# Attention and gated long convolution on one core: DMA transposes for the outputs of the later pairs, one cast for q and k, separate weight tiles for local pairs, and another order of the work

## Chip, core and metric

The kernel runs on one core of one Trainium2 chip. The metric is device time in microseconds; the kernel before takes 206.59 us (median of 3 runs, 206.18 to 206.97). Times of single operations below come from one profiled execution of it, whose span is 205.4 us. The engines are called PE (matmul; PEld is its weight loading), DVE (vector), ACT (scalar, with activation tables), POOL (GpSimd) and SP (the queue that issues most DMAs).

## What is computed

Batch 4, 8 heads, 768 positions, head width 64. Heads 0, 2 and 6 see all earlier positions ("full"); the others see the first 4 positions and a window of 64 ("local"). The attention output, heads side by side (768 x 512 for each batch), goes through a projection to three parts; the middle one is convolved circularly along the sequence with a filter, all three are multiplied, and the product is projected again.

```python
scores = scale * q @ k.T                  # masked: causal; local heads: sink or window
a = exp(scores - max); a = a / (sum(a) + 1e-9)
attn = a @ v                              # (B, H, S, D)
x = attn.transpose(0, 2, 1, 3).reshape(B, S, H * D)
x1, x2, x3 = split(x @ w_proj, 3)
x2_conv = irfft(rfft(x2, axis=1) * rfft(filter, axis=0), n=S, axis=1)
out = (x1 * x2_conv * x3) @ w_out
```

## The kernel before

**Units of work.** Two heads, h and h + 4, form a pair; the 16 pairs are numbered n = 0 to 15, four for each batch, in the order full-full, local-local, full-local, local-local (`PAIRS`, `KINDS`). Every step of a pair or a batch is a small named operation (`ops`), and the string `FAST` lists the names in the order in which they are issued. Each engine takes its own instructions in that order, and so does SP with its DMAs; there is no scheduler behind it. A suffix `/v`, `/s`, `/p` names the engine of a copy or an elementwise operation (DVE, ACT, POOL), and `@0` to `@3` names one of four PSUM slots of two banks. An operation waits, through semaphores, for what it reads and for the last users of the buffer that it writes.

**A pair.** `lq`, `lk`, `lv` load q, k and v from SP. `cq`, `ck`, `cv` cast to bf16 (`ev`, L963 to L971, makes all such copies). For n < 8 (`TURNED`) `T` transposes q and k on PE (L1340) and `E` copies them out of PSUM; from pair 8 on `T` is one DMA transpose from SP (L1350). `kx`, `ks`, `vx`, `vs` build the short key and value tiles of local heads. `sc` computes a chunk of scores (L1385; chunks n.0 to n.5 for full pairs, n.0 to n.2 for local, n.0 to n.4 for mixed ones); for the first four pairs `sb` adds the mask on PE (L1398), later `mk` and `mr` multiply it in on DVE. `ex` takes the exponential of a chunk on ACT into the weight tile `pT` (L1404). `at` is the weighted sum for one of the two heads (L1449), `rec` and `nm` divide by the row sum (L1455, L1463, L1466). `tn` transposes the pair's output, six 128 x 128 blocks, on PE (L1522), and `te` copies the blocks from PSUM to `xT`. `fd`, `fe` and, from pair 8, `fA`, `fS`, `fb`, `fr` fold the output for the transform; `W` transforms it (L1502 to L1510) and `We` copies it to `xh`.

**A batch.** `X` multiplies the transformed output with the middle part of the projection (L1553, six halves of four 128 x 512 matmuls), `Xe` copies that out, `pa`, `pb`, `pc` and the swap `sw` (a DMA from SP) multiply by the filter's spectrum. `x1` and `x3` are the two outer parts (L1588, half tiles of four 128 x 384 matmuls), `xs` and `g` take them up. `c` transforms back (L1618, halves of three 128 x 384 matmuls), `ce`, `cv` and `y` finish the convolution and the product. `o` is the output projection (L1645), `oe` its eviction, `st` the store. All four pairs of a batch must be in `xT` before its first `x1` or `x3` matmul.

**Setup.** `sin`, `cos`, `turns`, `angle`, `wrap` compute the transform tables; `lfilt`, `fold`, `F`, `H` the filter's spectrum; `lw0.*`, `lw1.*`, `lw2.*` load the three parts of the projection weights and `lwo` the output weights, all as casting DMAs from POOL. `blank` issues matmuls on zeros at the start. ACT loads an activation table where its function set changes.

**Buffers.** q and k tiles, key tiles and value tiles rotate over three, `pT` over two (even pairs one, odd pairs, which are the local ones, the other).

Of the kernel before, what the change touches and what calls it, by code (L numbers as in the profile page):

```python
# [10 lines left out]
BF16 = mybir.dt.bfloat16  # L11
# [16 lines left out]
W = 512  # L28
# [86 lines left out]
TURNED_BACK = (0, 1, 2, 3, 4, 5, 6, 7, 8, 9, 10, 11, 12, 13, 14, 15)  # L115
# [793 lines left out]
def patterned(  # L909
# [55 lines left out]
    def ev(out, in_):  # L965
        if now["engine"] == "v":
            nc.vector.tensor_copy(out=out, in_=in_)  # L967
        elif now["engine"] == "p":
            nc.gpsimd.tensor_copy(out=out, in_=in_)  # L969
        else:  # L970
            nc.scalar.copy(out=out, in_=in_)  # L971
# [795 lines left out]
```

## Time and profile before

| | |
|---|---|
| median of 3 runs | 206.59 us |
| profiled execution, span | 205.4 us |
| busy: PE, DVE, ACT, POOL | 183.4, 161.0, 143.8, 81.5 us |
| share of 16 DMA engines, hardware queue | 57.6% |
| score exponentials on ACT (68) | 59.8 us |
| x1 and x3 matmuls on PE (256) | 48.3 us |
| transposes of attention outputs on PE (96) | 7.8 us |

A stretch of the profile gives the time for which each engine was busy in it; matmuls are pipelined and overlap, so a busy PE is not PE at its peak. The chain of waits goes back from the last instruction, at each step to what released it. An idle engine costs nothing unless that chain passes through its wait.

### The profile page before, as it was taken

The page shows a single profiled execution, that of the slowest core. Times are in us where ns is not written, and L with a number is a line of the kernel's source. Part 1 is how long each engine was busy: PE and PEld are TensorE (multiplying, and loading weights), DVE is VectorE, ACT ScalarE, POOL GpSimd, SP SyncE. Part 2 cuts the span into 40 slices and gives each one's busy share as a digit, 9 for nine tenths or more (in the row PEclk, how much of TensorE's full clock was granted, in tenths as well). Part 3 has the DMA queues.
Part 4 walks back from the last instruction along what each step waited for, and adds up shares of the span by engine and source line. Part 5 has one row for each costly group of instructions (what it writes and reads, how often), then busy time and mean ns, then how long its engine had stood idle before and what let it go on. Part 6 is the DMA issues. An engine that isn't in the chain of part 4 may idle for free.

```text
span 205.4 us, 4423 instructions
## 1 busy us (share of the span) xinstructions
PE 183.4 (89%) x1718; PEld 107.1 (52%) x1718; DVE 161.0 (78%) x296; ACT 143.8 (70%) x199; POOL 81.5 (40%) x106
## 2 busy tenths in 40 slices
PE   0993999979699779989999999999999999999990
PEld 0443576545346355535655666555655866545540
DVE  4384563967678799988989998899999988689850
ACT  3959779959788958699939889666897623424521
POOL 3739716564050420192174326203354595040600
PEclk9997579999999999999999999999999999999997
DMA  5999999999923979901999998152013200022174
GB/s 160 305 303 341 198 265 226 257 238 261 238 59 79 229 150 217 223 3 49 277 221 233 231 269 161 37 118 49 5 66 142 105 0 2 3 51 102 73 292 162
DMA packets 74159, 32.87 MB, mean 160 GB/s; under 512 B 63507, under 2 KB 70419, under 8 KB 74131
## 3 DMA queue, kind: packets, MB, share of 16 engines
q1 hardware_dynamic: 71186, 29.63, 57.6%
q0 software_dynamic: 2944, 2.88, 8.3%
q8 instruction: 15, 0.25, 0.5%
q14 instruction: 14, 0.11, 0.2%
HBM read 24.64 MB, written 6.29 MB: 151 GB/s over the span
## 4 chain that ended last, share of the span: by engine, by line
PE 63%; ACT 16%; DVE 15%; issue 2%; DMA 1%; ACTq 0%; DVEq 0%
PE f_x_ps L1588 15%; PE f_X_ps L1553 10%; PE f_out_ps L1645 9%; PE f_c_ps L1618 7%; PE f_sc L1385 6%; ACT f_pT L1404 5%; PE f_att L1449 4%; PE f_blank_ps L1010 3%; DVE f_attn L1466 3%; PE f_qkT_ps L1340 2%; ACT f_qkT L971 2%; DVE f_fo L974 2%; ACT f_HAB L1205 2%; PE f_xt_ps L1522 2%; PE f_W_ps L1510 2%
## 5 line engine op out<-in xcount | busy, mean ns | idle before, releaser
L1404 ACT ACTIVATE f_pT<-f_sc 128x1024 bf16<-128x1024 f32 (+3 forms) x68 | 59.8, 921 | 7.2 <-PE f_sc L1385 5.1
L1588 PE MATMUL f_x_ps<-f_xT,f_wproj 128*128 128x384 bf16 x256 | 48.3, 327 | 1.0 <-ACT f_pT L1404 0.5
L1588 PEld LDWEIGHTS <-f_wproj 128*128 128x128 bf16 x256 | 23.1, 98 | 17.7 <-issue 2.6
L1385 PE MATMUL f_sc<-f_qkT 64*128 64x128 bf16 (+3 forms) x248 | 23.1, 258 | 1.9 <-DVE f_attn L1466 0.9
L974 POOL TENSOR_TENSOR f_fo<-f_attn 128x384 bf16<-128x384 bf16 x15 | 15.7, 1062 | 19.0 <-DVE f_attn L1466 12.7
L1645 PE MATMUL f_out_ps<-f_wout,f_gy 128*128 128x512 bf16 x96 | 22.9, 380 | 0.0
L1553 PE MATMUL f_X_ps<-f_wproj,f_xh 128*128 128x512 bf16 x96 | 22.7, 380 | 0.0
L974 POOL TENSOR_TENSOR f_gy<-f_conv,f_gy 128x768 bf16<-128x768 bf16 x7 | 11.5, 1668 | 22.9 <-issue 13.2
L1629 DVE TENSOR_TENSOR f_conv<-f_evs,f_c_ps 128x384 bf16<-128x384 f32 x32 | 16.4, 548 | 3.2 <-ACT f_evs L971 2.0
L1449 PEld LDWEIGHTS <-f_pT 128*128 128x128 bf16 x472 | 17.5, 101 | 2.5 <-DVE f_attn L1466 0.6
L1385 PEld LDWEIGHTS <-f_qkT 64*128 64x128 bf16 x248 | 10.4, 95 | 15.8 <-issue 12.3
L1618 PE MATMUL f_c_ps<-f_Gi,f_P 128*128 128x384 bf16 x96 | 18.2, 325 | 0.4 <-ACT f_evs L971 0.2
L1449 PE MATMUL f_att<-f_v_aug,f_pT 128*128 128x65 bf16 x392 | 18.2, 199 | 0.2 <-DVE f_attn L1466 0.2
L971 ACT CAST f_x1s<-f_x_ps 128x768 bf16<-128x768 f32 x14 | 11.3, 810 | 8.2 <-PE f_x_ps L1588 6.5
L969 POOL COPY f_v_x<-f_v_aug 64x520 bf16<-64x520 bf16 (+1 forms) x15 | 9.7, 648 | 18.5 <-ACT f_v_aug L971 11.0
L1340 PE MATMUL f_qkT_ps<-f_identity,f_qk_bf 128*128 128x128 bf16 x96 | 9.0, 242 | 8.6 <-ACT f_qk_bf L971 5.6
L967 DVE COPY f_qkT<-f_qkT_ps 128x768 bf16<-128x768 bf16 x7 | 6.7, 957 | 12.6 <-ACT f_qkT L971 6.3
L971 ACT COPY f_evs<-f_c_ps 128x384 f32<-128x384 f32 x16 | 7.7, 480 | 11.7 <-PE f_c_ps L1618 10.8
L1466 DVE TENSOR_TENSOR f_attn<-f_att,f_rec 128x768 bf16<-128x768 f32 x15 | 14.3, 956 | 1.1 <-DVE f_rec L1455 0.5
L1645 PEld LDWEIGHTS <-f_gy 128*128 128x128 bf16 x96 | 8.9, 98 | 10.2 <-issue 0.3
L971 ACT COPY f_o<-f_out_ps 128x1024 f32<-128x1024 f32 (+1 forms) x11 | 9.7, 907 | 6.2 <-PE f_out_ps L1645 6.2
L1553 PEld LDWEIGHTS <-f_xh 128*128 128x128 bf16 x96 | 8.9, 98 | 9.9 <-issue 0.4
(128 smaller groups left out, 354.9 us busy)
## 6 DMA issues: line engine op xcount, KB each, us to landing
f_v_f<-in_v_dram SPq DMA_DIRECT2D x32, 192.0 KB, 4.7
out_dram<-f_o SPq DMA_DIRECT2D x9, 512.0 KB, 3.1
f_qk_f<-in_k_dram SPq DMA_DIRECT2D x5, 384.0 KB, 5.5
f_qk_f<-in_q_dram SPq DMA_DIRECT2D x5, 384.0 KB, 4.8
f_qk_f<-in_q_dram SPq DMA_DIRECT2D x10, 192.0 KB, 4.2
f_qk_f<-in_k_dram SPq DMA_DIRECT2D x10, 192.0 KB, 4.0
f_wproj<-in_moe_w_proj_dram POOLq DMA_DIRECT2D x6, 256.0 KB, 12.0
out_dram<-f_o SPq DMA_DIRECT2D x6, 256.0 KB, 3.6
```

What stands on the lines that cost most here:

```text
L971: nc.scalar.copy(out=out, in_=in_)
L974: (nc.gpsimd if now["engine"] == "p" else nc.vector).tensor_tensor(out, a, b, op)
L1340: nc.tensor.transpose(ps[:, a, t * 128:(t + 1) * 128], qk_bf(n)[:, a, t].rearrange("p hh d -> p (hh d)"), identity())
L1385: nc.tensor.matmul(sc[:, bank, col:col + 128 * cnt], lhsT=keys, rhs=qkT(n)[rows, 0, 128 * i:128 * (i + cnt)], start=(col == 0 or not biase ...
L1404: nc.scalar.activation(out=pT(n)[:, c, :, 0:w], in_=held[f"sc.{n}.{c}"][:, :, 0:w], func=AF.Exp, scale=SCALE)
L1449: nc.tensor.matmul(att[:, hh, 65 * i:65 * i + 65], lhsT=pT(n)[:, c, bank, col:col + 128], rhs=values, start=(z == 0), stop=(z == len(here) ...
L1466: nc.vector.tensor_mul(attn(n).rearrange("p i hh d -> p hh i d"), rows[:, :, :, 0:64], held[f"rec.{n}"][:, :, :, None].to_broadcast([128, ...
L1553: nc.tensor.matmul(ps[:, u, :], lhsT=xh(b)[:, cc, chain, 128 * part:128 * part + 128], rhs=wproj()[:, cc, DM:2 * DM], start=(cc == 0), sto ...
L1588: nc.tensor.matmul(ps[:, s, 0:HS], lhsT=wproj()[:, cc, part * DM + cb * 128:part * DM + (cb + 1) * 128], rhs=xT(b)[:, cc, s * HS:s * HS + HS],
L1618: nc.tensor.matmul(ps[:, r, 0:HS], lhsT=P(b)[:, t, u, ch], rhs=Gi()[:, tile_no], start=(m == 0), stop=(m == 2))
L1629: fn(conv[:, half * HS:half * HS + HS], held[f"evs.{b}.{cb}"], held[f"c_ps.{b}.{cb}"][:, 1, 0:HS])
L1645: nc.tensor.matmul(ps[:, i % 2, :], lhsT=gy(b)[:, cb, i * 128:(i + 1) * 128], rhs=wout()[:, cb, :], start=(cb == 0), stop=(cb == NC - 1))
```

## The change

- `TURNED_BACK` loses pairs 8 to 14. For these seven `tn` is one DMA transpose from SP, from the attention output straight to `xT`, and `te` is gone; pairs 0 to 7 and 15 keep PE.
- For pairs 8 to 15 the loads of q and k write a layout with the two heads beside each other, and one `cqk` casts both in one flat copy of 128 x 1536, in place of `cq` and `ck` of 128 x 768 each with a rearranged source.
- `pT` of local pairs is a tile of half the size, and two of them alternate; full and mixed pairs share the other.
- `ev` has a letter `d`, a plain DMA from SP; the new list uses it for `vs2`, `ks15`, `vx13` and `vx15`. An operation `exp0` takes the exponential of one column. `APART` is empty and has no effect.
- `FAST` is another list throughout, with other engines for many copies and other places for the loads.

```diff
-TURNED_BACK = (0, 1, 2, 3, 4, 5, 6, 7, 8, 9, 10, 11, 12, 13, 14, 15)
+TURNED_BACK = (0, 1, 2, 3, 4, 5, 6, 7, 15)
...
+        elif now["engine"] == "d":
+            nc.sync.dma_start(out=out, in_=in_)
...
+    @op("exp0")
+    def _():
+        nc.scalar.activation(out=table(), in_=table(), func=AF.Exp)
...
     def pT(n):
-        return buf(f"pT.{n}", [128, 6, 2, W], BF16, f"pT{n % 2}")
+        if KINDS[PAIRS[n % HP]] == "LL":
+            return buf(f"pT.{n}", [128, 3, 2, W], BF16, f"pTl{n // 2 % 2}")
+        return buf(f"pT.{n}", [128, 6, 2, W], BF16, "pT0")
...
-                            nc.sync.dma_start(out=qk[:, a, hh],
+                            nc.sync.dma_start(out=qk.rearrange("p a h t d -> p (a h t d)").rearrange(
+                                                  "p (a t h d) -> p a t h d", a=2, t=NT, d=D)[:, a, :, hh],
...
+        if n >= TURNED:
+            @op(f"cqk{n}")
+            def _(n=n):
+                ev(qk_bf(n).rearrange("p a t h d -> p (a t h d)"),
+                   held[f"qk_f32.{n}"].rearrange("p a h t d -> p (a h t d)"))
```

The branch that `tn` of pairs 8 to 14 now takes was in the code before:

```python
nc.sync.dma_start_transpose(out=xT(b)[:, hp, :].rearrange("p (t s) -> p t s", t=NT),
                            in_=attn(n).rearrange("p t hh d -> p (t hh d)"))
```

Of the new list, the start, the stretch with the weights' loads, and the stretch around the outputs of pairs 8 to 11:

```diff
+mblank blank0@0 fcol1 par mtab0 lk1 table sin0 tcol tfrac ck0/s lq2 fcol0 turns2 angle0 ident ones1 T0.1@1 quarter
+mtab2 blank1@2 angle2 angle1 turns1 wrap1 turns0 lq1 wrap2 cq0/s E0.1/s T0.0 lk2 cq1/p wrap0 lk3 sin1 size kz0
+cq2/v E0.0/v T2.0@3 T1.0@0 sc0.3@2 sin2 E1.0/v cos1 mtab1 mtab3 btab blank2@1 E2.0/s ck1/v cos2 sb0.3 ex0.3 ck2/p
...
+cv3/v cv2/p vs2/d exp0 lk4 vx2/v ex2.2 ex2.0 at1.0@1 at1.1 rec1 nm1/v tn0@2 te0/v W0.1@3 Gh0 W0.0 sc2.1@0 sb2.1
...
+vs5/p lv4 lw0.1 X0.1.1@2 sc4.2@1 sc4.3@3 ex4.3 lw0.0 X0.1.0 pa0.0/v mk4.2 ex4.2 mk4.1 lw2.1 lw2.0 T6.0@0 E6.0/s
...
+cv0.1.1 We4/s cv0.1.0 c0.0.0 ce0.0/v cqk10/s cv0.0.0 at6.0@0 cv0.0.1 T10 T9 vx6/p vs6/p at6.1 rec6 sc8.3@3 ex8.3
+c0.3.1@1 nm6/v c0.3.0 lwo ce0.3/s y0.1/p sc8.2@2 ex8.2 y0.0/p cv0.3.0 cv0.3.1 y0.3/p c0.2.0@3 c0.2.1 fd6/p sc8.4@0
+ce0.2/s sc8.0@2 vs7/v ex8.0 x30.3.1@1 x30.3.0 cv0.2.0 lk12 cv0.2.1 y0.2/v tn6@2 ex8.4 te6/s at7.0@3 lq12 g0.3 at7.1
+lk11 o0.1.0@0 sc8.5@2 ex8.5 rec7 kx9/v sc8.1@1 fe6/v nm7/v mk8.2 fd7/v ex8.1 mk8.0 o0.0.0 mk8.1 o0.1.1 o0.0.1
...
+mk11.2 mk11.1 x31.0.1 T12 We8/s sc12.0@0 sc12.5@3 rec10 nm10/v fe10/p fd10/v ex12.0 tn9 x11.2.0@2 x11.2.1 g1.0
+xs1.2/s lk13 at11.1@0 fr9 ex12.5 at11.0 rec11 x31.1.0@1 tn10 sc12.4@2 sc12.1@3 nm11/v x31.1.1 W9.0@0 lk15 pc1.2/v
+ex12.4 g1.1 tn11 W9.1 x31.2.1@2 ex12.1 We9/s mk12.2 sc12.2@1 fA10/v sc12.3@3 lq14 fS10/v fe11/p fr10 fd11/v ex12.2
+x31.2.0 g1.2 fA11/p c1.1.0@0 fb10/v fS11/v ex12.3 x12.0.0@1 pb1.0/v pc1.0/v x12.0.1 xs2.0/s x32.0.1@2 x32.0.0
+fb11/v fr11 W10.0@3 W10.1 ce1.1/s c1.1.1 g2.0 cv1.1.0 We10/s lq13 cqk13/p lv12 lk14 cv1.1.1 c1.0.0@1 c1.0.1 ce1.0/v
+cv1.0.1 cv1.0.0 W11.1@2 cv13/s W11.0 We11/s cv12/s cqk14/s T13 cqk15/p y1.1/v mk12.0 T14 y1.0/v c1.2.1@3 c1.2.0 T15
+mk12.1 ks15/d cv14/v c1.3.1@0 ce1.2/s cv1.2.0 c1.3.0 X2.0.1@1 ce1.3/s ks13/p cv1.3.1 cv1.3.0 X2.0.0 Xe2.0/s lv15
```

The same instructions as before remain otherwise: the same score, weighted-sum, projection and transform matmuls, and 17 blank ones.

121 lines of the change are left out of this document (52 added, 69 removed).

## The prediction

> **What bounds the kernel now.** I read the spans first, then the busy time by stretches, then the chain of waits.
>
> ```profile
> core 0: 205.4 us, clock 0.968
> 0.00:92.20 92.20, 75.71 (x757) 44.43 (x758) 65.01 (x121) 73.28 (x105) 41.17 (x63) 0.94 0.92 209
> 92.20:200.30 108.10, 107.65 (x963) 62.65 (x962) 95.96 (x176) 70.00 (x95) 40.33 (x44) 1.00 0.46 118
> 92.20 3.56 PE f_out_ps L1645 x16
> 195.02 5.19 PE f_out_ps L1645 x24
> 200.28 0.59 ACT f_o L971
> ```
>
> The columns of the two stretches are length, then busy us and count of PE, PEld, DVE, ACT, POOL, then granted clock, DMA share, GB/s. I cut at 92.2 us, where the first output matmuls of batch 0 stand, because the new list has them after almost the same matmul work. Right of the cut PE is busy 107.65 of 108.10 us at full clock: only less work on PE, or a new wait, can move that part. The span then needs 5.1 us more for the last eviction and store, which stay as they are in kind. Left of the cut PE is busy 75.7 of 92.2 us, and its streaming is less than that. No engine is full; the chain of waits passes from one to the other:
>
> ```profile
> PE 63%; ACT 16%; DVE 15%; issue 2%; DMA 1%; ACTq 0%; DVEq 0%
> 3.40 1.28 ACT L971
> 17.59 1.28 ACT L1404
> 18.89 0.61 ACT f_pT L1404
> L1404 ACT ACTIVATE f_pT<-f_sc 128x1024 bf16<-128x1024 f32 (+3 forms) x37 | 32.9, 931 | 4.9 <-PE f_sc L1385 2.9 <-PE f_sc L1398 1.6
> 19.20:29.40 10.20, 9.87 (x107) 7.30 (x107) 4.86 (x12) 7.65 (x10) 5.42 (x11) 0.55 1.20 232
> ```
>
> ACT has 16% of the chain, 32.9 us, and hardly any of it can lie right of the cut, where PE never stops; so about 30 of ACT's 73.3 us there, 0.4 of them, set the pace. The first exponential starts only at 18.89. ACT also stands idle 4.9 us before exponentials, for scores. From 19.2 to 29.4 the array is granted 0.55 of its clock.
>
> **Work taken off the first 92 us.** I counted in both lists what stands ahead of the first output matmul.
>
> ```profile
> L971 ACT CAST f_qk_bf<-f_qk_f 128x768 bf16<-128x768 f32 x6 | 5.1, 848 | 0.0
> L1205 ACT ACTIVATE f_HAB<-f_F_ps 128x512 bf16<-128x512 f32 (+2 forms) x7 | 5.3, 791 | 3.1 <-DVE f_HAB L1203 2.2 <-PE f_F_ps L1196 0.9
> L1463 ACT ACTIVATE f_attn<-f_att,f_rec 128x64 bf16<-128x64 f32 x12 | 2.6, 346 | 0.2 <-DVE f_rec L1455 0.2
> L971 ACT CAST f_X<-f_X_ps 128x1024 bf16<-128x1024 f32 x1 | 1.0, 1012 | 0.2 <-PE f_X_ps L1553 0.2
> L971 ACT COPY f_evs<-f_c_ps 128x384 f32<-128x384 f32 x4 | 1.9, 480 | 1.8 <-PE f_c_ps L1618 1.8
> L971 ACT COPY f_Gi<-f_Gi_ps 128x768 bf16<-128x768 bf16 x1 | 0.8, 804 | 0.0
> L969 POOL CAST f_qk_bf<-f_qk_f 128x768 bf16<-128x768 f32 x5 | 4.4, 878 | 1.2 <-DMA f_qk_f<-in_q_dram 1.1
> ```
>
> ACT's q and k casts go from 9 to 3 plus one of double width: 6 x 0.85 less, about 1.5 more (an estimate, twice 0.85 less one start), so -3.6. Of 8 filter scalings 3 stay, about -4.1. Pair 5's normalisation in 12 pieces goes to DVE, -2.6. One inverse eviction (0.48) and one table eviction (0.8) go. Added are one each of a q/k eviction, a spectrum eviction, an output eviction and an x1 eviction, a wide X cast (1.0), an exponential, and small copies: 5.6. Sum -5.9. The compiled new program also loads two activation tables where the old one loads three, -1.28, and that one lies on the chain for certain. What goes elsewhere: DVE +1.3, POOL +3.9 (its casts at 0.88 each), both engines with idle time left of the cut.
>
> The bounds: -7.2 us if every microsecond counts, 0 if DVE and POOL take up the pace. I take the chain's share, 0.4 x 5.9 = 2.4, plus 1.3 for the table load, less 0.3 for DVE's 1.3 by its own share of the chain: -3.4.
>
> **Score chunks grouped, local weight tiles of their own.** Chunks of one pair now stand two or three together on PE, and pairs 1, 3, 5 and so on alternate between two weight tiles. ACT's 4.9 us of waiting for scores is all that this can give; it gives nothing if the four PSUM slots still meter the scores. Some waits are at the very start, so I take a bit over a third: -1.8. It removes no instruction.
>
> **Outputs transposed by DMA.**
>
> ```profile
> L1522 PE MATMUL f_xt_ps<-f_identity,f_attn 128*128 128x128 bf16 x96 | 7.8, 219 | 0.9 <-DVE f_gy L1607 0.7
> 98.59 0.33 PE f_xt_ps L1522 x6
> L967 DVE COPY f_xT<-f_xt_ps 128x768 bf16<-128x768 bf16 x10 | 5.4, 544 | 1.0 <-PE f_xt_ps L1522 1.0
> ```
>
> Seven groups of six transposes leave PE, each 0.33 us on the chain: 7 x 0.33 = -2.3, all of it right of the cut where PE is the bound, so it counts in full. The seven evictions (0.54 each on DVE) lie beside PE work there and count nothing by themselves; should DVE fall behind they are worth up to 3.8.
>
> In their place stand seven DMA transposes on SP, each waiting for a normalisation, with loads queued behind.
>
> ```profile
> L1350 SPq DMA_TRANSPOSE f_qkT<-f_qk_bf x8: 1399/1843/2803, 66.2 to 135.4; - x8
> DMA to landing us min/median/max: 3.7/4.1/6.3
> f_qk_f<-in_q_dram SPq DMA_DIRECT2D x10, 192.0 KB, 4.2
> f_Xw<-f_X SPq DMA_DIRECT2D x8, 128.0 KB, 2.9
> L1466 DVE TENSOR_TENSOR f_attn<-f_att,f_rec 128x768 bf16<-128x768 f32 x15 | 14.3, 956 | 1.1 <-DVE f_rec L1455 0.5
> 112.10 1.95 PE f_x_ps L1588 x12
> 140.44 0.97 PE f_c_ps L1618 x6
> 141.41 0.62 PE f_sc L1385 x16
> 177.09 5.18 PE f_X_ps L1553 x24
> L1455 DVE RECIPROCAL f_rec<-f_att 128x12 f32<-128x12 f32 x16 | 3.6, 226 | 1.2 <-PE f_att L1449 1.2
> ```
>
> The old trace has no such transpose. Its size is half that of the q/k one, so it lands between 2.9 (the nearest smaller transfer) and 4.1 us; I take 3.5. The tightest user is `x12.0.0`, which needs pair 11's. Between the last matmul of `at11` and it the new list has four half tiles of x (16 matmuls at 1.95/12 = 0.163, 2.6 us), an inverse half (3 at 0.97/6, 0.5), two W halves (by their 1280 columns at the x rate, 0.54) and four score chunks of a pair with full heads (30 blocks at 0.62/16, 1.2): 4.8 us. The path needs the reciprocal 0.23, the normalisation 0.96 and 3.5, so 4.7, and SP may still be sending `tn10` and `lk15`, another 0 to 1.9. I take 0.8.
>
> Behind `tn11` SP sends `lq14` and `lq13`, then POOL casts `cqk13`, SP sends `T13`, POOL copies `kx13`, and `sc13.0` follows. From the end of pair 11's normalisation: about 0.9 for `tn11` on SP, 1.2 for `lq14`, 4.2 for `lq13` to land, 1.65 cast, 4.1 transpose, 0.6 copy, 12.7 in all. PE has until `sc13.0` eight half tiles of x (5.2), eight inverse halves (3.9), four spectrum halves (16 at 5.18/24, 3.5), six W halves (1.6) and four score chunks (1.2), 15.4 us less the 1.2 of reciprocal and normalisation: 14.2. So nothing at the medians; with transposes at 6.3 and 2.8 in place of 4.1 and 1.84, and a slower load, up to 4.0. I take 0.7. All new waits on SP here: 0 to 5.8, taken 1.5.
>
> **Weights later.** `lwo` moves from 33.6 us to just behind pair 6's `vs6`.
>
> ```profile
> L1180 POOL DMA_DIRECT2D f_wout<-in_moe_w_out_dram x1: 783/783/783, 33.6 to 33.6; - x1
> f_wout<-in_moe_w_out_dram POOLq DMA_DIRECT2D x1, 512.0 KB, 8.1
> f_wproj<-in_moe_w_proj_dram POOLq DMA_DIRECT2D x6, 256.0 KB, 12.0
> ```
>
> From `at6.1`, which needs `vs6`, to the first output matmul PE has 5.7 us of work (three weighted sums, four score chunks, four inverse halves, two half tiles of x and a group of transposes); the weights land 8.1 us after issue. So 0 to 2.5 late, taken 1.0. The projection weights for x1 and x3 also move, behind `vs5` on POOL, with some 14 us of PE work before their use against 12.0: nothing, or 2 us should they land last. The bare `exp0` costs 0.2 us of ACT and comes after real exponentials.
>
> **Sum.** 205.4 - 3.4 - 1.8 - 2.3 + 1.5 + 1.0 = 200.4 for a profiled execution. The median of the runs shown is 206.59, 1.2 above the profile's span, so **201.6 us**.
>
> **Rivals.**
> 1. The clock stays up. The row 19.20:29.40 shows 10.2 us at about half rate, with 5.1 us of full-rate work. Between 13.0 and 19.2 the array had been busy under half of the time:
>
> ```profile
> 13.00:19.20 6.20, 2.93 (x38) 0.91 1.12 371
> ```
>
> The new list sends eight blank matmuls before any transpose, and its first scores come before the last six blanks, so the same work could meet a full clock. Then -5.1 is won as well, and all of ACT's -7.2 may count: 205.4 - 7.2 - 5.1 - 2.3 + 2.5 + 1.2 = 194.5. Against it: with blanks first, the array may wait again behind evictions and cool as before. The Trainium skill ("TensorE: Matmul & The Clock Gate", Part 1) says that the array falls to half rate after an idle window of about 3.4 us and recovers after a busy one; the trace agrees, with a half-rate stretch of 10.2 us after a thin 6.2. By that rule the new prologue decides which of the two it is, and 194.5 would hold if no window is idle.
> 2. Only the transposes count: DVE and POOL take the pace as ACT lets go. 205.4 - 2.3 + 1.2 = 204.3. For it: POOL takes 3.9 us more, and the chain already passes between engines. Against it: ACT's table load lies alone on the chain.
> 3. Slower: SP is a queue in order, and waiting instructions in it hold back loads. `vs2` as a DMA waits for `cv2` (load 4.7, cast 0.9) with pair 4's loads behind it, up to 5.6, of which I count half (3.0) since ACT has other work; the transposes of pairs 8 to 11 hold the loads of 13 to 15, 5.8 at the worst, of which two thirds, 3.9, are counted; and the first part then keeps only the table load's 1.3. 205.4 - 1.3 - 2.3 + 3.0 + 3.9 + 1.2 = 209.9. It decides once the holds pass 6.5 us in all, which is what the forecast's gains come to (3.4 + 1.8 + 2.3 - 1.0).
>
> ```profile
> f_v_f<-in_v_dram SPq DMA_DIRECT2D x32, 192.0 KB, 4.7
> ```
>
> For it speaks the chain to `sc13.0`, with 1.5 us to spare; against it, the DMA share of 0.46 right of the cut.
> 4. The change doesn't do what it says: the relief of ACT is replaced by equal waits, 206.6.
>
> **Chances.** Forecast 0.45, clock 0.13, transposes only 0.22, slower 0.16, none 0.04. A measurement of this kernel tells about 0.5% from no change, which is 205.6 to 207.6. The forecast and rivals 1 and 2 nearly all lie below: faster 0.76. Same 0.07 takes rival 4 and the near edges; slower 0.17. The range 195.0 to 208.0 leaves out half of rival 1 and most of rival 3, some 0.2. For the forecast alone it is 198 to 204.
>
> **What would show it.** Right: a first exponential before 16 us; two table loads; ACT busy some 66 to 68 us before the first output matmul and that matmul at 86 to 88 us; 54 transposes of outputs on PE instead of 96; PE busy nearly without a gap after that, for 105 us or so. Wrong: PE waiting long for DMA on x or output matmuls (late weights), on scores of 13 to 15 (SP's queue), DVE near full in the first half, or a second stretch of half clock. If the first output matmul stands where it stood, the main term has failed and about 204 is left.

## The result, and the profile after

| | before | after |
|---|---|---|
| median | 206.59 us (5 runs, 205.13 to 210.6) | 194.92 us (5 runs, 192.44 to 201.79) |
| ratio | | 0.9389 [0.9312, 0.9466] |
| DMA engines, hardware queue | 57.6% | 70.8% |

The kernel became 6.1% faster by the ratio and 11.7 us by the medians, which is 6.7 us more than forecast (201.6) and just below the range. Here and in the tables below the ratios leave out executions in the slower state (of the new kernel 201.79 and 198.01 us) and the medians do not, so that 11.7 us is 5.6% of 206.59 where the ratio says 6.1%. The profiled execution of the new kernel happened to be its longest (201.79 us, span 199.8); where a cleaner one is needed I read the first experiment, the new kernel without the operation `exp0` (195.61 us, span 193.5).

The stretches of the new kernel up to and after its first output matmul, and two short ones within; columns as in the prediction (length, then PE, PEld, DVE, ACT, POOL, granted clock, DMA share, GB/s):

```profile
core 0: 199.8 us, clock 0.956
0.00:84.20 84.20, 73.11 (x780) 44.04 (x781) 65.69 (x121) 66.65 (x88) 42.02 (x68) 0.94 1.02 208
84.20:194.50 110.30, 106.09 (x903) 60.61 (x899) 85.45 (x158) 71.53 (x94) 42.47 (x45) 0.97 0.69 146
110.00:115.00 5.00, 2.07 (x16) 0.93 (x14) 4.93 (x6) 2.53 (x4) 4.23 (x4) 0.90 1.05 170
115.00:121.80 6.80, 6.80 (x47) 3.67 (x46) 3.08 (x6) 2.53 (x4) 2.08 (x2) 0.57 0.60 106
```

The same of the new kernel without `exp0`:

```profile
core 0: 193.5 us, clock 0.989
0.00:80.20 80.20, 69.39 (x774) 42.45 (x780) 66.72 (x121) 67.01 (x87) 42.26 (x68) 1.00 1.05 219
80.20:188.00 107.80, 104.27 (x888) 60.24 (x896) 84.86 (x158) 70.97 (x93) 42.19 (x45) 0.98 0.69 149
104.00:108.00 4.00, 3.19 (x50) 2.10 (x48) 4.00 (x5) 3.00 (x5) 3.10 (x3) 1.00 0.97 160
108.00:112.00 4.00, 2.37 (x22) 1.65 (x23) 3.09 (x6) 1.43 (x2) 2.04 (x2) 0.83 0.63 109
```

The first output matmul stands at 84.2 us in the one and 80.2 in the other, against 92.1 before. ACT is busy 66.7 and 67.0 us ahead of it, as forecast (66 to 68), but the stretch is shorter by 12 us in the cleaner profile, not by the 4 to 6 of the forecast (86 to 88). Seven runs below keep the operations of this first part in their order (e3, e5, e11, e12, e13, e15, e18): in their profiles the matmul stands at 77.1 to 85.5 us, 80.5 in the middle, and in those of three runs with the old first part (e2, e4, e6) at 92.9 to 94.4, so a single profile tells the 12 us to a few. ACT's idle time in it fell with the work: 92.2 - 73.3 = 18.9 us before (at the prediction's cut), 80.2 - 67.0 = 13.2 after. What lies behind that matmul is not shorter: 205.4 - 92.1 = 113.3 us before, 193.5 - 80.2 = 113.3 after, although PE has less work there. The rest now has a hole at 104 to 112 us (PE busy 5.6 of 8 us) with a half-rate stretch behind it. The chain of that profile passes through the hole by way of DVE, which is busy for all of the first 4 us of it (more under "What holds the middle?"). Below, the chain of waits of the new kernel, and its waits of PE (total, times, longest):

```profile
PE 52%; DMA 17%; DVE 14%; issue 4%; SPq 4%; ACT 4%; POOL 3%; DVEq 0%
```

```profile
PE f_qkT_ps L1354 <- POOL f_qk_bf L967: 2.7, 2, 2.5
PE f_x_ps L1602 <- DMA f_wproj<-in_moe_w_proj_dram: 2.7, 1, 2.7
PE f_x_ps L1602 <- DVE f_attn L1480: 1.9, 1, 1.9
PE f_sc L1399 <- DMA f_qkT<-f_qk_bf: 1.0, 1, 1.0
PE f_W_ps L1524 <- POOL f_fo L974: 1.0, 1, 1.0
```

ACT has gone from 16% of the chain to 4%, DMA from 1% to 17%. Which part of the change did it cannot be read from here.

### The profile page after: what moved, and what is told of

Same layout as the page of the kernel before. It is cut to its first block, busy times and chain, and to the rows that moved or that the text cites. A ratio compares the mean times of both kernels' runs of the same rounds, so it can differ in the third digit from the quotient of the medians.

```text
span 199.8 us, 4326 instructions
## 1 busy us (share of the span) xinstructions
PE 179.2 (90%) x1676; PEld 104.7 (52%) x1676; DVE 151.1 (76%) x278; ACT 138.7 (69%) x181; POOL 84.5 (42%) x112
## 3 DMA queue, kind: packets, MB, share of 16 engines
q1 hardware_dynamic: 77746, 31.18, 70.8%
## 4 chain that ended last, share of the span: by engine, by line
PE 52%; DMA 17%; DVE 14%; issue 4%; SPq 4%; ACT 4%; POOL 3%; DVEq 0%
PE f_x_ps L1602 14%; PE f_out_ps L1659 9%; PE f_X_ps L1567 8%; DMA f_Xw<-f_X 6%; PE f_c_ps L1632 6%; DMA f_qkT<-f_qk_bf 6%; DMA f_qk_f<-in_q_dram 5%; PE f_sc L1399 4%; PE f_att L1463 4%; DVE f_pT L1438 2%; DVE f_P L974 2%; ACT f_pT L1418 2%; POOL f_gy L974 2%; SPq L1311 2%; SPq L1308 1%
## 5 line engine op out<-in xcount | busy, mean ns | idle before, releaser
L1602 PE MATMUL f_x_ps<-f_xT,f_wproj 128*128 128x384 bf16 x256 | 49.9, 341 | 4.6 <-DMA f_wproj<-in_moe_w_proj_dram 2.7
L1602 PEld LDWEIGHTS <-f_wproj 128*128 128x128 bf16 x256 | 24.5, 101 | 22.4 <-issue 6.2
L1399 PE MATMUL f_sc<-f_qkT 64*128 64x128 bf16 (+3 forms) x248 | 21.3, 261 | 1.7 <-DMA f_qkT<-f_qk_bf 1.0
L971 ACT COPY f_o<-f_out_ps 128x1024 f32<-128x1024 f32 (+1 forms) x13 | 10.9, 849 | 10.1 <-PE f_out_ps L1659 9.5
L971 ACT CAST f_x1s<-f_x_ps 128x768 bf16<-128x768 f32 x16 | 12.9, 808 | 7.0 <-PE f_x_ps L1602 7.0
L967 POOL CAST f_qk_bf<-f_qk_f 128x768 bf16<-128x768 f32 (+1 forms) x10 | 10.4, 1048 | 14.7 <-DMA f_qk_f<-in_q_dram 7.8
L971 ACT CAST f_X<-f_X_ps 128x1024 bf16<-128x1024 f32 x11 | 11.2, 1020 | 5.4 <-PE f_X_ps L1567 5.4
L1438 DVE TENSOR_TENSOR f_pT<-f_pT,f_mtab 128x1024 bf16<-128x1024 bf16 (+1 forms) x18 | 14.8, 836 | 0.1
L971 ACT CAST f_xh<-f_W_ps 128x768 bf16<-128x768 f32 x14 | 11.1, 799 | 5.3 <-PE f_W_ps L1524 3.2
L967 POOL COPY f_kx<-f_qkT 128x16 bf16<-128x16 bf16 (+3 forms) x14 | 4.6, 338 | 22.2 <-DMA f_qkT<-f_qk_bf 13.2
```

Of the source, the lines that this page charges most:

```text
L1399: nc.tensor.matmul(sc[:, bank, col:col + 128 * cnt], lhsT=keys, rhs=qkT(n)[rows, 0, 128 * i:128 * (i + cnt)], start=(col == 0 or not biase ...
L1438: nc.vector.tensor_mul(some, some, near(c)[:, None].to_broadcast([128, 2, cols, 128]))
L1602: nc.tensor.matmul(ps[:, s, 0:HS], lhsT=wproj()[:, cc, part * DM + cb * 128:part * DM + (cb + 1) * 128], rhs=xT(b)[:, cc, s * HS:s * HS + HS],
```

## Experiments

Ratios are against the kernel before, on the same chip; "the new kernel" is at 0.9389. Where a list is spliced, PSUM slots that would have been taken are renamed (at most 3).

### Is the clock the gain? The start

Four runs touch the start: the bare exponential (at 27 us in the new kernel), the blank matmuls in the new and in the old kernel, and the third table load.

```diff
e1_no_exp0:   -... cv2/p vs2/d exp0 lk4 ...        +... cv2/p vs2/d lk4 ...
e7, e16:      -for i, count in enumerate((8, 3, 6)):   +for i, count in enumerate((1, 1, 1)):
e8:           -table sin0 tcol tfrac ck0/s ... cq0/s   +table tcol tfrac ck0/s ... cq0/s sin0
```

> The changed kernel without the one-column exponential (0.2 us of ACT, after real exponentials). Every theory: the same as the changed kernel, 193 to 195 us against 206.6 before, ratio 0.93 to 0.95. If that little instruction forces something (a table load, a wait), it moves by over 1 us. It also gives a second profile of the new order, in which waits for DMA may be shorter than in the first one (17% of its chain).

> The new kernel with 3 blank matmuls instead of 17, one at each place. Theory, the clock: without them the array comes up later and the work between 9 and 20 us runs at half rate; the old trace shows what that costs, 5.1 us of full-rate work in 10.2 us, so 198 to 200 us against 195 and a half-rate stretch beginning before 20 us. Rival: the array waits for transposes and casts in that time anyway, so that blanks and clock cost nothing: 194.5 to 196 us.

> The old kernel with 3 blank matmuls instead of 17. Before, the transposes of the second loaded pair stand behind 11 blank ones (3.47 us, from 9.44 on), and ACT waits 2.12 us for them at 11.5 us. Theory, the blanks themselves make the old start late: 204.5 to 205.5 us. Rival, the array then is cold for longer, or the exponentials wait for casts anyway: 206 to 208 us.

> The new kernel with the first sine moved behind the casts of pair 0, so that ACT loads three activation tables instead of two, the middle one between the cast of q and the first copy of the transposed tiles. Theory: that load (1.28 us in the old trace) lies on the chain and costs all of it: 196 to 197 us against 195. Rival: it is hidden beside other work of the start: within 0.5 us of the new kernel.

Measured: without `exp0` 195.61 us, 0.9479 [0.9433, 0.9526]; with few blanks 195.54, 0.9444 [0.9298, 0.959]; the old kernel with few blanks 207.33 beside 207.5; three tables 196.95, with runs from 191.28 to 199.87, too wide for a ratio. `exp0` does nothing that can be told. With few blanks the first record of full clock is at 20.2 us, against 9.4 in the run without `exp0` (a group of six transposes takes 0.85 us in the first row below, 0.50 in the second, from the run without `exp0`), and the end does not move: the first weighted sum comes at 20.8 us instead of 19.0, but the first spectrum matmul at 44.7 and 44.9, and the spans of the two profiles are 193.2 and 193.5 us.

```profile
13.36 0.85 PE L1354 MATMUL f_qkT_ps<-f_identity,f_qk_bf 128*128 128x128 bf16 x6
```

```profile
13.90 0.50 PE L1348 MATMUL f_qkT_ps<-f_identity,f_qk_bf 128*128 128x128 bf16 x6
```

With three tables ACT's first exponential starts at 14.47 us, without (second fence, from the run without `exp0`) at 14.09:

```profile
7.79 1.28 ACT L1016 ACT_TABLE_LOAD   x1
...
13.18 1.28 ACT L1416 ACT_TABLE_LOAD   x1
14.47 8.12 ACT L1416 ACTIVATE f_pT<-f_sc 128x768 bf16<-128x768 f32 x10
```

```profile
12.39 1.28 ACT L1412 ACT_TABLE_LOAD   x1
14.09 8.37 ACT L1412 ACTIVATE f_pT<-f_sc 128x768 bf16<-128x768 f32 x10 [0.42 <-PE f_sc L1406]
```

So 0.4 us of the 1.28 is left on the way to the first exponential, since other work of the start was not ready earlier. Neither the clock of the start, nor the blanks, nor the table load by itself is the gain.

The clock's price over a whole run can be estimated from the kernel before, which ran 59 times beside the experiments and whose clock varies by itself. Span times (1 - mean clock) is the full-rate time lost (the time ahead of the first clock record is not in it). Of the 45 runs within 1.5% of the shortest beside the same experiment 15 lost about 3.5 us (median 205.41 us), 15 about 5.1 (206.39), 15 about 6.6 (207.21): 3.1 us of lost rate go with 1.8 us of time, 0.6 us for each. A straight line through all 59 gives 0.9, and one through the 21 runs of the new kernel, e1, e8, e15 and e17 gives 1.1. The new kernel's shorter three runs lost 0.6 to 2.7, 1.0 in the middle; 4.1 us less lost than 5.1 is then worth 2.5 to 4.5 us, an estimate from these groups. That the lost rate is the cause, and not another sign of the same waits, they do not show.

### The half-size weight tiles alone

```diff
     def pT(n):
-        return buf(f"pT.{n}", [128, 6, 2, W], BF16, f"pT{n % 2}")
+        if KINDS[PAIRS[n % HP]] == "LL":
+            return buf(f"pT.{n}", [128, 3, 2, W], BF16, f"pTl{n // 2 % 2}")
+        return buf(f"pT.{n}", [128, 6, 2, W], BF16, "pT0")
```

> The kernel before with two half-size weight tiles for the local pairs and nothing else. Theory A (the order alone can use them, since the old list never issues a local pair's exponentials ahead of the previous local pair's sums): 206.6, within 0.5. Rival D (the old order waited for the shared tile): 1 us less or more.

207.61 us, 0.9947 [0.99, 0.9993]: at most 1% by themselves, in the old order.

### What are the DMA transposes worth?

In the old kernel alone (e2: the seven `tn` on SP at their old places, `te` gone); in the new kernel undone (e3: the seven on PE, with evictions, some slots renamed); and then the pieces of that undoing: the slots alone (e13), the slots and PE groups whose result nobody reads (e11), and evictions of those too (e12).

```diff
e2:   -TURNED_BACK = (0, ..., 15)                  +TURNED_BACK = (0, 1, 2, 3, 4, 5, 6, 7, 15)
e3:   -TURNED_BACK = (0, 1, 2, 3, 4, 5, 6, 7, 15)  +TURNED_BACK = (0, ..., 15), tn8@1 te8/v ... tn14@0 te14/v
e13:  17 names with another @slot, nothing else
e11:  e13, and behind each tn8 to tn14 a tx on PE
e12:  e11, and behind each tx a ty/v (pairs 8 to 11, 14) or ty/s (12, 13)
```

> The kernel before with one part alone: outputs of pairs 8 to 14 transposed by DMA, their seven evictions gone, the old order otherwise. Theory A (the order makes most of the gain; PE is the bound in the second part, so seven groups at 0.33 us count): 2.3 us less, 204.3, unless a transpose lands too late for its x matmuls. Rival B (these transposes make most of the 12 us, by freeing PSUM slots, DVE and ACT too): 198 or less. Rival C (in the old order SP's waits and late landings eat it): 206.6 or more.

> The changed kernel with that part undone: outputs of pairs 8 to 14 on PE again, evicted on DVE (ACT for pairs 12 and 13), PSUM slots renamed where they collide. Theory A: 2.3 to 4 us over the changed kernel, 196 to 198. Rival B: 201 or more. Rival C (DMA transposes cost as much as they give): the same as the changed kernel or less.

> The new kernel with the 17 PSUM slots renamed as in the two runs with extra transposes, and nothing else. It tells what of their 5.7 us is the slots' and what the matmuls'. Theory 1, the matmuls (2.3 us of streaming and the waits behind them): 195 to 196 us here. Theory 2, the slots, which make matmuls wait for other evictions: 198 to 201 us.

> The new kernel, which keeps the seven DMA transposes, with the seven PE transpose groups put back beside them (into a PSUM slot that nobody reads; slots as in the run with the outputs back on PE). It prices PE's share of them alone: 7 x 0.33 = 2.3 us by my forecast, 197.3 to 198.3 us against 195.3. Rival: PE has slack in the new order, no change, 195 to 196. If it costs over 4 us, the PSUM slots or the order behind the groups count, not the matmuls.

> As the run before this one, and the seven evictions as well, to a tile that nobody reads (five on DVE, two on ACT). Theory: DVE is close to the bound in the new order (it waits in PE's place at the new kernel's normalisations), so the evictions, which I counted at nothing with up to 3.8 us should DVE fall behind, cost that: 200.5 to 203 us, as much as with the outputs back on PE for real (202.98). Rival: the evictions are hidden, 197.3 to 198.5 us, and the 7.4 us that going back to PE costs come from something else, such as the later arrival of the transposed outputs.

| run | median us | ratio |
|---|---|---|
| e2, old order, DMA transposes | 217.33 | 1.0515 [1.0454, 1.0577] |
| new kernel without `exp0` | 195.61 | 0.9479 [0.9433, 0.9526] |
| e13, slots | 198.8 | 0.9641 [0.9552, 0.973] |
| e11, slots and PE groups | 201.3 | 0.9768 [0.9697, 0.9838] |
| e12, and evictions | 202.1 | 0.9832 [0.9739, 0.9925] |
| e3, on PE instead of DMA | 202.98 | 0.9807 [0.9751, 0.9863] |

By medians, the seven PE groups cost 201.3 - 198.8 = 2.5 us, the evictions 0.8, and the slots 198.8 - 195.6 = 3.2; the intervals of the first two steps overlap, that of the slots does not. The profiles agree: behind the first output matmul the run without `exp0` takes 113.3 us, e13 194.0 - 77.1 = 116.9, e11 199.2 - 80.5 = 118.7, e12 198.5 - 78.5 = 120.0, which puts the slots at 3.6, the PE groups at 1.8 and the evictions at 1.3. In e13 PE waits for evictions of x1 and of a spectrum half that it does not wait for so long without the renaming (there 0.5 us for x1):

```profile
PE f_x_ps L1600 <- ACT f_x1s L969: 1.1, 1, 1.1
...
PE f_att L1461 <- ACT f_x1s L969: 0.9, 1, 0.9
PE f_X_ps L1565 <- ACT f_X L969: 0.7, 1, 0.7
```

My theories for e11 and e12 were both half right: PE's share is about the 2.3 us of the forecast, the evictions are nearly hidden, and the largest part of the 7.4 us that undoing the transposes seemed to cost (202.98 against 195.61) is that the slots did not fit any more.

In the old order the same seven transposes cost 10.7 us (217.33 against 206.59). The profile is of that run's longest execution (223.28 us, the others 216.41 to 218.18), so its waits may be longer than in the others. This is the tile `f_xT` on SP's queue in that run (form and number, then who waited for it, with us and times), two of PE's waits, and a piece of the chain of waits:

```profile
L1526 SPq DMA_TRANSPOSE f_xT<-f_attn x7: 1211/1280/2437, 125.3 to 177.6; - x7
...
  DVE f_attn L1461: 9.7, 2
  PE f_x_ps L1583: 2.5, 2
```

```profile
PE f_sc L1380 <- DVE f_attn L1461: 8.2, 2, 7.3
...
PE f_x_ps L1583 <- DMA f_xT<-f_attn: 2.5, 2, 2.0
```

```profile
125.34 2.44 SPq L1526
...
127.83 2.72 DMA f_xT<-f_attn
...
130.64 0.97 DVE f_attn L1461
```

The output tile `attn` rotates over two. A transpose on PE releases it at once; one that stands in SP's queue holds it until its turn, and the normalisation of the pair after next, which writes the same tile, waits: 9.7 us on DVE, and PE waits 8.2 us for that normalisation. The chain comes to the transpose at 125.34 through SP's loads, swaps and a store from 118.80 on, and goes on through its landing to that normalisation. Less than a third as much is the wait that I had priced, of x for the transposed output. In the new order nobody waits for `f_xT` in the run without `exp0`.

### Where in the list does the gain lie?

Both lists have done nearly the same operations when the first output matmul stands (all but 9 names of the new one and 5 of the old). So they can be spliced there: e5 takes the new list up to that matmul and what is left of the old one behind it (outputs on PE), e6 the reverse, e14 the new list only up to the first spectrum matmul, e18 is e5 with DMA transposes in the old rest. A pair has `cqk` where its casts lie on the new side.

```diff
-FAST = new
+FAST = new[:first "o0"] + [x for x in old if x not in new[:first "o0"]]      # e5, e18
+FAST = old[:first "o0"] + [x for x in new if x not in old[:first "o0"]]      # e6
+FAST = new[:first "X0"] + [x for x in old if x not in new[:first "X0"]]      # e14
```

> The new list up to the first output matmul of batch 0 (447 operations), then what is left of the old list in its old order, with all outputs transposed on PE and the old casts where they lie in that rest. The two lists have done almost the same work by that point. Theory 1, the gain lies ahead of that matmul (in one trace of the new order without the bare exponential it stands at 81.1 us against 92.2 before, 11 us earlier, while the rest took 112.4 against 113.2): 9 to 11 us less than before, 196 to 198 us. Theory 2, the gain is spread and the DMA transposes with the list around them carry most of it (going back to PE for them cost 7.4 us): the first part alone gives 11.2 - 7.4 = 3.8 us, so about 203 us. My forecast's own terms ahead of that matmul, -3.4 - 1.8 + 1.0, would give 202.6. An in-between figure of 199 to 201 would say that each has a part.

> The reverse: the old list up to its first output matmul, then what is left of the new list, with DMA transposes for the outputs of pairs 8 to 14. Theory 1: the rest gives only about 1 us, 205 to 206 us. Theory 2: it gives the 7.4 us, 199 to 200 us. My forecast's terms right of that point, -2.3 + 1.5, would give 206.0. Rival: the new rest relies on loads and casts that the old start has not made, and with SP holding loads behind its new waits the time goes over 207.

> The new list up to the first spectrum matmul of batch 0 (253 operations), then what is left of the old list in its old order, with all outputs on PE. In the traces that matmul starts at 55.0 us before and at 44.9 in the new order, 10 us earlier. Theory 1, the lead is made at the start and kept: 196.5 to 199 us. Theory 2, it is lost again, because later work in the old order waits for loads or for DVE whatever the start: over 202 us. The run with the new list up to the first output matmul gave 201.3.

> The run with the new list up to the first output matmul and the old rest (201.33 us), now with DMA transposes for the outputs of pairs 8 to 14 in the old rest, evictions gone. Theory 1, the transposes are worth their PE time wherever PE is the bound: 2.3 us less, 199 us. Theory 2, a DMA transpose needs the new rest around it, since in the old order the seven cost 10.7 us: 205 us or more.

| run | median us | ratio |
|---|---|---|
| e5, new first, old rest, outputs on PE | 201.33 | 0.9797 [0.9687, 0.9908] |
| e6, old first, new rest | 206.39 | 1.003 [0.9978, 1.0082] |
| e14, new up to the spectrum, old rest | 203.56 | 0.9818 [0.9736, 0.99] |
| e18, e5 with DMA transposes | 207.99 | 1.0032 [0.9981, 1.0082] |

Neither theory of e5 and e6 holds; my forecast's own terms for the two parts, 202.6 and 206.0, are near both (201.33, with a loss at the splice in it that is shown below, and 206.39). The parts do not add: 2.0% from the new first part, nothing from the new rest, 6.1% from both. In e14 most of the lead is lost early, as its second theory said: PE waits 3.3 us for a cast of q and k on DVE at 47 us, right behind the splice, the first output matmul comes at 88.5, 3.6 us ahead of before, and these stay to the end (201.7 - 88.5 = 113.2). In the profiles e5 shows how a lead is lost and kept. Stretches of e5:

```profile
0.00:78.90 78.90, 69.03 (x784) 42.08 (x784) 66.84 (x121) 67.30 (x89) 42.41 (x69) 1.00 1.05 227
...
84.00:88.00 4.00, 1.15 (x7) 0.39 (x4) 2.43 (x5) 1.99 (x5) 0.91 (x2) 1.00 1.14 304
104.00:108.00 4.00, 4.00 (x43) 2.45 (x39) 3.93 (x9) 3.41 (x6) 2.57 (x3) 1.00 1.30 227
108.00:112.00 4.00, 4.00 (x67) 2.89 (x65) 3.88 (x9) 3.88 (x6) 0.00 (x0) 1.00 1.15 300
```

Stretches of the kernel before, 8 us later:

```profile
112.00:116.00 4.00, 4.00 (x43) 2.44 (x39) 3.93 (x9) 3.41 (x6) 2.58 (x3) 1.00 1.14 241
116.00:120.00 4.00, 4.00 (x67) 2.90 (x66) 3.88 (x9) 3.86 (x6) 0.01 (x1) 1.00 0.94 224
```

The last two rows of e5 are the rows of before, engine by engine, 8 us ahead, and the spans differ by the same (205.4 - 197.3 = 8.1): once in step, the old rest keeps a lead to the end. But of the 13 us that e5 had at its first output matmul (78.9 against 92.1; five operations that the old list has done by then lie behind it, nine others are done), 5 were gone by 104 us. At 84 to 88 PE is busy 1.15 of 4 us, and DVE, then PE, wait:

```profile
DVE f_qk_bf L965 <- DMA f_qk_f<-in_k_dram: 4.2, 1, 4.2
```

```profile
PE f_xt_ps L1537 <- DVE f_attn L1481: 2.9, 1, 2.9
```

```profile
81.19 1.47 SPq L1311 DMA_DIRECT2D f_qk_f<-in_k_dram  x2
85.53 0.56 DVE L965 CAST f_qk_bf<-f_qk_f 128x768 bf16<-128x768 f32 x1 [4.15 <-DMA f_qk_f<-in_k_dram]
```

That k is pair 11's. Its load, `lk11`, is the last operation of the new part, since the new list casts it only 56 operations later (`cqk11`). The old list loads it 149 operations ahead of its cast `ck11`; in e5 there are 14 between them, and the cast holds DVE, with the normalisation of `attn` behind it. So at least this hole is made by the splice: two lists that each fit their own loads do not fit each other, and e5 makes the new first part look worth less than it is. No run moved that load, so how much less stays open.

e18 is 6.7 us slower than e5 by medians, 4.9 by the ratios. The old rest has no place for the transposes even after the new start: in the profile of e18 (its longest execution, 214.23 us) DVE waits 3.7 us for the tile `attn` and PE 2.4 for the transposed output, as in e2, but PE also waits 5.3 us for `f_wproj`.

### Order or engines?

Ahead of the first output matmul 62 operations that both lists have changed their engine. e9 is the new kernel with these on their old engines, e10 the old kernel with 61 of them on their new ones.

```diff
e9:   cq2/v -> cq2/s, E1.0/v -> E1.0/s, ck1/v -> ck1/p, ..., nm5/v -> nm5/s, y0.2/v -> y0.2/p   (in the new order)
e10:  cq2/s -> cq2/v, E1.0/s -> E1.0/v, ck1/p -> ck1/v, ..., nm5/s -> nm5/v, y0.2/p -> y0.2/v   (in the old order)
```

> The new order with the old engines: of the operations that stand ahead of the first output matmul in both lists, 62 change their engine, and here they are put back (15 of them from DVE to ACT, 3 from POOL to ACT, 11 from ACT to DVE, the others between DVE and POOL; pair 5's normalisation in 12 pieces and the filter scalings are among them). ACT then has about 5 us more ahead of that matmul. Theory 1, the relief of ACT makes the first part shorter, and counts almost in full: 4 to 6 us more than the new kernel, 199.5 to 201.5 us. Theory 2, the order itself does it: within 2 us of the new kernel, 195 to 197 us. My forecast's share of 0.4 would give 197.

> The reverse in the old kernel: 61 of these operations on their new engine, in the old order (the copy that became a DMA stays where it was). Theory 1: 4 to 6 us less than before, 201 to 203 us. Theory 2: 205.5 to 207 us, no change. Rival: in the old order the new engines are late where the old ones were not, over 207.5 us.

e9: 227.82 us, 1.1047 [1.0941, 1.1153]. e10: 209.28 us, 1.0101 [1.0041, 1.0162]. Both theories fall, and with them the way in which I had priced the first part. Stretches up to the first output matmul, of e10, and then of e9 with some of its waits of PE:

```profile
0.00:91.30 91.30, 73.24 (x756) 42.88 (x756) 67.35 (x120) 67.29 (x89) 42.24 (x67) 0.96 0.95 211
```

```profile
0.00:116.10 116.10, 82.53 (x781) 48.30 (x782) 70.40 (x122) 72.23 (x104) 39.28 (x63) 0.87 0.77 163
```

```profile
PE f_W_ps L1522 <- DVE f_xT L963: 4.7, 1, 4.7
PE f_qkT_ps L1352 <- DVE f_qk_bf L963: 4.3, 1, 4.3
...
PE f_att L1461 <- DVE f_v_x L963: 3.7, 1, 3.7
PE f_qkT_ps L1352 <- ACT f_qk_bf L969: 3.4, 2, 2.9
```

In e10 ACT is relieved by the whole 5.9 us (67.3 busy instead of 73.2), and the first output matmul comes at 91.3 instead of 92.1: ACT's idle time rose from 18.9 to 24.0 us and took nearly all of it. In e9 ACT has 5 us more to do than in the new kernel (72.2 against 67.0), and the matmul comes 36 us later, at a mean clock of 0.87. Each engine takes its list in order, so an operation that changes its engine also moves behind other ones and ahead of others; order and engines are one plan.

### What holds the middle?

The new kernel without the stores of batch 0 (e15, its output block is not written), and with the weights issued earlier (e17).

```diff
e15:  -st0.1, st0.3, st0.5
e17:  -vs5/p lv4 lw0.1 X0.1.1@2 ... lw0.0 ... lw2.1 lw2.0 T6.0@0     ... c0.3.0 lwo ce0.3/s
      +... lw1.0 lw0.1 lw0.0 at3.1@0 ... We2/v lw2.1 lw2.0 ... lwo T6.0@0
```

> The new kernel without the three stores of batch 0, so that its first output block stays unwritten: 1.6 MB less for the DMA engines, which would have moved between 88 and 110 us. In the new order their mean busy share is 1.05 from 81 to 130 us (0.76 in the like stretch before), transposes of q and k take 5.2 to 7.3 us to land where the chain passes through them, and two runs whose array works at different times stand together again at 116 us. Theory, the DMA engines are the bound there: 2 to 4 us less, 191.5 to 193.5 us. Rival, the landings are long only where nobody waits: 194.7 to 196.

> The new kernel with the loads of the weights for x1 and x3 issued behind the last load of the middle part and behind the third transformed output, and that of the output weights ahead of pair 6's transposes, all some 8 us earlier on POOL. In two profiles of the new order PE waits 2.7 and 2.9 us for f_wproj at the first x matmul, in another 0.8 us for f_wout. Theory, late weights cost what I counted (1.0) or what those rows show: 1 to 3 us less than the new kernel, 192 to 194.5 us. Rival, the time up to 116 us is set elsewhere, and earlier weights only push the loads of q, k and v back: 195 to 198 us.

e15: 194.58 us, 0.9374 [0.9296, 0.9452]; 1 us at the most for 1.6 MB (194.92 and 195.61 with the stores), so the DMA engines are busy there but their throughput is not the bound. e17: 194.32 us, 0.9383 [0.9304, 0.9462], its runs from 191.46 to 195.3: not to be told from the new kernel's 0.9389. Its profile, however, has no hole in the rest:

```profile
core 0: 189.7 us, clock 0.993
81.50:184.00 102.50, 102.48 (x901) 59.70 (x897) 84.47 (x158) 71.32 (x93) 42.51 (x45) 1.00 0.67 150
104.00:108.00 4.00, 4.00 (x55) 2.61 (x54) 3.58 (x7) 3.77 (x6) 2.85 (x2) 1.00 1.17 194
```

That is the shortest span of all the profiles. What fills the hole in the other runs can be read from DVE and POOL. There DVE multiplies masks into two weight chunks, ahead of the normalisation for which PE waits, and POOL multiplies by the spectrum; the first two rows are of the run without `exp0`, the other two of e17:

```profile
104.87 3.57 DVE L1432 TENSOR_TENSOR f_pT<-f_pT,f_mtab 128x768 bf16<-128x768 bf16 x2
104.82 2.13 POOL L972 TENSOR_TENSOR f_P<-f_X,f_HAB 128x1024 bf16<-128x1024 bf16 x1 [4.32 <-ACT f_X L969]
```

```profile
104.25 1.16 DVE L1436 TENSOR_TENSOR f_pT<-f_pT,f_mtab 128x768 bf16<-128x768 bf16 x2
105.15 2.24 POOL L972 TENSOR_TENSOR f_P<-f_X,f_HAB 128x1024 bf16<-128x1024 bf16 x1 [4.49 <-ACT f_X L969]
```

The same two operations of DVE take 2.4 us longer where POOL's multiplication begins with them. Of the 2.4 us for which PE idles in the hole, 1.7 end with the normalisation behind these two and 0.7 with pair 12's transposed q and k. In the new kernel's profile (3.55 us, POOL 0.55 ahead) and in e15 (3.08, POOL 0.16 behind the start) it is as in the run without `exp0`; in e7, whose profile has no hole either (PE busy 8.0 us from 104 to 112), and in e13 (both 1.15, POOL 0.9 and 1.1 behind) it is as in e17. So e17's profile owes this to how the two engines happened to meet in that execution, of which the earlier weights may or may not be the reason; no run moved either operation. Nothing tried here is shown to beat the new kernel.

## Why the prediction was right or wrong

The sign held, and so did the count of work taken off ACT and PE; the size did not: 11.7 us where 5.0 were forecast.

- **ACT's relief, -3.4, and the grouped scores, -1.8: this is the step that failed.** The work taken off ACT was counted well (66.7 to 67.0 us busy ahead of the first output matmul, forecast 66 to 68), and the first exponential came at 14.1 us in the cleaner profile (16.9 in the new kernel's own). What failed is to price the part by ACT's share of the chain of the old order, as if work were taken off and the rest stayed where it was. With the old order the relief is worth 0.8 us in the profiles at that matmul (e10), and no gain in the time; with the new order and the new engines that matmul comes 12 us earlier (92.1 to 80.2), 6.2 by less ACT work and 5.7 by less ACT idle time, where the sum had -5.2 for it; 4.8 of them are there at the first exponential already (18.9 to 14.1). My bounds for this part, 0 and -7.2 with up to -4.9 for the scores, did hold it; the value taken from between them was the wrong one.
- **One table load fewer, -1.28 "for certain":** wrong by itself. With three tables the first exponential moves by 0.4 us, and the first weighted sum stands at 19.1 us against 19.0.
- **Transposes off PE, -2.3:** the size was about right; seven groups put back cost 2.5 us beyond the slots by medians, 1.8 by the profiles. That the evictions count nothing was nearly right (0.8 and 1.3).
- **New waits on SP, +1.5:** wrong in place. Neither pair 11's landing at `x12.0.0` nor the chain to `sc13.0` appears among PE's waits in the run without `exp0`. The hole is 20 us of work ahead, around `x31` and pair 12's scores: 2.4 us of idle PE at 104 to 112 us, and some 1.7 for the 3.4 us at half rate behind it, in the cleaner profile; about 4 us in all, inside my bound of 5.8, but only 0.7 of it is a wait for a DMA of SP's queue: DVE is late there beside POOL, where I had counted the work moved to the two engines by their idle time alone. I missed altogether that a transpose in SP's queue holds the tile `attn`; the new list avoids it, the old one does not (e2, e18).
- **Late weights, +1.0:** of that size where it occurs; PE waits 2.7 us for `f_wproj` in the new kernel's profile, 0.8 for the output weights in e7, not at all in the run without `exp0`.
- **Rival 1, the clock stays up:** its time, 194.5, came out, in part by luck. In the run without `exp0` the array indeed runs at full clock from 9.4 up to 111.8 us; yet e7, cold until 20.2 us, is as fast, and over whole runs less lost rate goes with some 2.5 to 4.5 of the 11.7 us. I had charged the half-rate stretch of the start alone with all of its 5.1. The other half of the rival, "all of ACT's -7.2 may count", is nearer to what was found.
- **Rivals 2 and 4** fell with the time. **Rival 3**, SP's queue making it slower, is what happens to the transposes without the rest of the list (217.33 and 207.99 us): a real mechanism, which the new order was made to go round.

The sum failed for one reason: it added up parts that do not add. The new first part alone is worth 2.0% (with the loss at e5's splice in it), the new rest alone nothing, the transposes alone -5.2%, the engines alone -1.0%, the tiles alone 0.5%; together 6.1%. What in detail lets the new rest gain 4% only behind the new start is shown as far as the seam of e5, which the splice itself makes, and the fit of the slots (e13), and stays open beyond that. The flat cast `cqk` with its layout and the four copies by plain DMA had no run of their own.

## What to carry to other kernels

In a list that each engine takes in order, order, engines, buffers and the places of the loads are one plan: a part costed alone can be worth nothing or have the other sign, and the share of the chain in the old order says little about what the work is worth in a new one; better to count how much idle time beside it can go, and to give such a part its whole range. Before moving a transpose to a DMA queue, look at what its source tile blocks: with two tiles in rotation it was the next writer that waited, not the reader. In e7 a cold array at the start, where PE had idle time to spare, cost nothing that can be told; look where the clock is low before putting a price on it. And look at what two engines do at the same time before giving one of them the other's work: here DVE was slower beside POOL.

## What was not expected of the hardware

The array's half-rate stretches between two of full rate came in lengths of 3.4, 6.8 and 10.2 us in all these profiles, and in different places in different executions: the new kernel's profile has one at 12.6 us, that of the run without `exp0` none before 111.8. The Trainium skill ("TensorE: Matmul & The Clock Gate", Part 1) gives a free-running window of about 3.4 us, in which the granted rate is decided; these lengths, one, two and three times that, agree.

DMA transposes of 128 x 768 elements from one tile to another hold SP for 1.2 to 2.6 us each. In the run without `exp0` (first fence) they land after 4.1 us in the median, in e6 (old first part, new rest) after 2.9, though the mean DMA share over the time in which they are issued is 0.81 in both; what makes the difference is not shown:

```profile
DMA to landing us min/median/max: 2.8/4.1/5.5
```

```profile
DMA to landing us min/median/max: 2.5/2.9/4.2
```

Seventeen PSUM slots renamed, with the order, the engines and the work the same, cost 3.2 us by medians and 3.6 by the profiles: which slot a matmul writes decides whose eviction it waits for, as the rows of e13 show.

DVE's multiplications of masks into the weights take the same time everywhere as long as POOL is not multiplying, casting or copying beside them: over all 20 profiles the 190 of 128 x 1024 that stand alone take 0.68 to 0.69 us, the 50 beside POOL up to 2.6. Why is not shown.
